# One core, sparse attention feeding a feed-forward layer: a head of feed-forward steps for the second chunk, and two small adds moved from GpSimd to VectorE

## The chip, the cores and the metric

The kernel runs on one core of a Trainium2 chip, as one program. The metric is device time in microseconds (us) of one execution. The core's engines run side by side, each taking its own instructions in order: TensorE (PE in the rows, its weight loads PEld), VectorE (DVE), ScalarE (ACT), GpSimd (POOL) and SyncE (SP, which here only issues DMAs).

## The reference, cut to what matters

Attention of 4 batches x 8 heads over 768 positions of 64, where a query sees 4 sink positions and a window of 128; then a feed-forward layer 512 -> 2048 -> 512 on all 3072 tokens, with a piecewise quadratic in the middle.

```python
scores = np.matmul(q, k.transpose(0, 1, 3, 2)) / np.sqrt(D)
scores = np.where(is_sink | in_window, scores, -1e9)
a = np.exp(scores - np.max(scores, axis=-1, keepdims=True))
a = a / (np.sum(a, axis=-1, keepdims=True) + 1e-09)
x = np.matmul(a, v)                   # then heads side by side: 3072 x 512
h = x @ w_in
g = np.where(h >= 1, h, np.where(h <= -1, 0, (h + 1) ** 2 / 4))
out = g @ w_out
```

## The kernel before

The tokens are cut into eight chunks of 384 (a batch, first or second half). A chunk's attention is eight units, one for each head; its feed-forward work is `moe_steps`: four `split` steps (the chunk's activations as a rounded part, ScalarE L596, and a rest, VectorE L597), then for each of 16 blocks `j` four steps `stage1` (L566, twelve matmuls into one PSUM bank `h_ps`, of which there are two) and, two blocks behind, three steps `stage2` (L585). Between them a block's values pass L573, L574 (ScalarE), L575 (VectorE), L576 (ScalarE) and L577 (GpSimd in chunk 0, VectorE later).

Every matmul operand is such a pair of a rounded part and a rest. The weights arrive as 64-bit words and are decoded once, in 16 weight steps, each a DMA (L199) and four VectorE passes over 128 x 1024 with a ScalarE cast ahead of the last: L164, L170, L173, cast L174, L177. Four of them lie in `first_pairs`, the attention of chunk 0, and twelve are spread over chunk 0's feed-forward steps. Below, "weight step 15" is the sixteenth and last; its destination is the last `w` of the decode, and weight step 14's is `wi_150`.

The loop at L641 builds, for chunk c, the list of attention steps of chunk c and of feed-forward steps of chunk c - 1, merged by `spread` in proportion to weights. In pass c == 1 the attention list is four pairs of heads of `pair_steps` (chunk 1, on 64-row operands: scores L422, transposes L455 and L457, sums L486, values L474), and after it the first "native" units, 16 and 17, of chunk 2. TensorE runs exactly in the order in which steps are called (`manual_schedule`). For the other engines a scheduler, at build time, decides the order from its own estimates, so that an edit of the list moves their instructions too.

A native unit's softmax: `scores` (L277) for three query tiles, maximum and shift on VectorE (L281), exponent on ScalarE (L284, which also sums), the 1e-9 on GpSimd (L289), the reciprocal (L290), the two weighted passes (L296, L298), the sink part (L301), all on VectorE; then TensorE's transposes L336 (tiles) and L337 (sinks). GpSimd also forms the rests of the queries (L263), for units 16 to 19 those of the keys (L261), of the values (L314), and of the block values in chunk 0 (L577).

Of the kernel before, what the change touches and what calls it, by code (L numbers as in the profile page):

```python
# [13 lines left out]
ALU = mybir.AluOpType  # L14
# [5 lines left out]
CT = 3  # L20
NSINK = 4
KB = P + NSINK
NCT = DM // P
# [5 lines left out]
NATIVE = 16  # L29
# [11 lines left out]
LEAD = 0.9  # L41
# [8 lines left out]
def attn_ffn(ctx, tc, qk, qkp, vx, vs, par, w_in, w_out, out):  # L50
    nc = tc.nc
# [214 lines left out]
    def scores(u, i):  # L266
        b, h, t0 = u
        qs, k_s = st["qk", u]
        if i == 0:
            st["p", u] = [att.tile([P, CT, 260], F32, name="p"), att.tile([P, 2 * CT], F32, name="stat")]  # L270
        p, stat = st["p", u]
        t = t0 + i
        lo = KB if t == 0 else 0
        c0 = i * KB if t0 else max(0, (i - 1) * KB)
        ps = ps_a.tile([P, 512], F32, name="ps_a")
        for j, q in enumerate(qs):
            nc.tensor.matmul(ps[:, lo:260], lhsT=q[:, i * P:(i + 1) * P], rhs=k_s[:, c0:c0 + 260 - lo],  # L277
                             start=(j == 0), stop=(j == len(qs) - 1))
        peak_i = peak[:, units.index(u), i:i + 1]
        m = (m0, m1, m2)[min(t, 2)]  # L280
        nc.vector.tensor_tensor_reduce(  # L281
            out=p[:, i, lo:260], in0=ps[:, lo:260], in1=m, scale=-0.125, scalar=3.0e38,
            op0=ALU.add, op1=ALU.min, accum_out=peak_i)
        nc.scalar.activation(p[:, i, lo:260], p[:, i, lo:260], AF.Exp, bias=peak_i, scale=-1.0,  # L284
                             accum_out=stat[:, i:i + 1])
        if i < CT - 1:
            return
        st.pop(("qk", u))
        nc.gpsimd.tensor_scalar(stat[:, CT:2 * CT], stat[:, 0:CT], 1.0e-9, None, op0=ALU.add)  # L289
        nc.vector.reciprocal(stat[:, CT:2 * CT], stat[:, CT:2 * CT])  # L290
        i0 = int(t0 == 0)

        for i in range(CT):
            r, own = stat[:, CT + i:CT + i + 1], p[:, i, KB:260]
            if t0 + i == 0:
                nc.vector.tensor_scalar(own, own, r, None, op0=ALU.mult)  # L296
            else:
                nc.vector.tensor_tensor_reduce(out=own, in0=own, in1=p[:, i, 0:P], scale=r, scalar=0.0,  # L298
                                               op0=ALU.add, op1=ALU.add, accum_out=stat[:, i:i + 1])
        sk = att.tile([P, CT * NSINK], F32, name="sk")[:, :(CT - i0) * NSINK]  # L300
        nc.vector.tensor_tensor(sk.rearrange("p (i s) -> p i s", s=NSINK), p[:, i0:, P:KB],  # L301
                                stat[:, CT + i0:2 * CT].unsqueeze(2).broadcast_to([P, CT - i0, NSINK]), op=ALU.mult)
        st["p", u] = (p, sk)
# [186 lines left out]
    def pair_steps(m):  # L490

        a, b = 2 * m - 2, 2 * m - 1
        sc = [(0.45, lambda i=i: pair_scores(m, i)) for i in range(CT)] if m < NATIVE // 2 else [(0.0, lambda: None)] * CT
        steps = [(0.0, lambda: pair_load(m + 1))] if m + 1 < NATIVE // 2 else []
        if m < NATIVE // 2:
            steps.append((0.0, lambda: pair_values(m)))
        tp = [(0.35, lambda u=u, i=i: early_transp(u, i)) for u in (a, b) for i in range(2)]
        pv = [(0.65, lambda: pair_r(m - 1)), (1.2, lambda: pair_av(m - 1)())]
        dg = [(0.0, lambda: pair_sums(m))] if m < NATIVE // 2 else []
        if m % (H // 2) == 0:  # L500
            return steps + tp[:3] + sc[:1] + tp[3:] + pv[:1] + sc[1:2] + pv[1:] + sc[2:] + dg
        return steps + tp[:1] + sc[:1] + tp[1:] + sc[1:2] + pv + sc[2:] + dg
# [38 lines left out]
    units = [(b, h, t0) for b, t0 in chunks for h in range(H)]  # L541

    def attn_steps(n):
        us = {k: units[n - k] for k in (-1, 0, 1, 2) if 0 <= n - k < len(units)}
        steps = []
        if n == NATIVE:
            steps.append((0.0, lambda: load(us[0])))
        if -1 in us:
            steps.append((0.0, lambda: load(us[-1])))
        if 1 in us and n - 1 >= NATIVE:  # L550
            steps.append((0.0, lambda: values(us[1])))
        steps += [(0.22, lambda i=i: scores(us[0], i)) for i in range(CT) if 0 in us]
        steps += [(0.43, lambda: transp(us[1]))] if 1 in us and n - 1 >= NATIVE else []
        steps += [(1.0, lambda: av(us[2]))] if 2 in us and n - 2 >= NATIVE else []
        if n in CHECK:
            steps.append((0.0, lambda: recheck(n - CHECK[0], n)))
        return steps
# [41 lines left out]
    def moe_steps(row0, tail):  # L599

        x = xpool.tile([P, 2, NCT, CT * P], F32R, name="x")
        o_ps, hs = [], {}
        steps = [(0.0, lambda ct=ct: split(x, ct)) for ct in range(NCT)]
        second = tail[:]
        for j in range(NJ):
            if j < LAG:
                steps += second[j * CT:(j + 1) * CT]
            steps += [(0.49, lambda j=j, ct=ct: stage1(x, j, ct, hs, row0)) for ct in range(NCT)]
            if j >= LAG:
                steps += [(0.65, lambda j=j - LAG, tt=tt: stage2(o_ps, hs, j, tt, row0)) for tt in range(CT)]  # L610
        tail[:] = [(0.65, lambda j=j, tt=tt: stage2(o_ps, hs, j, tt, row0)) for j in range(NJ - LAG, NJ)
                   for tt in range(CT)]
        return steps

    def spread(a, b, lead=1.0):

        wa, wb = (sum(w for w, _ in s) for s in (a, b))
        steps, n, da, db = [], 0, 0.0, 0.0
        for step in b:
            while n < len(a) and da * lead * wb <= db * wa:  # L620
                steps.append(a[n])
                da += a[n][0]
                n += 1
            steps.append(step)
            db += step[0]
        return steps + a[n:]
# [14 lines left out]
    for c in range(len(chunks)):  # L641
        n1 = min(H * (c + 1), len(units)) + 2
        if c == 1:
            attn = [step for m in range(5, 9) for step in pair_steps(m)]
            attn += [step for n in range(NATIVE, n1) for step in attn_steps(n)]
        elif c > 1:
            attn = [step for n in range(n0, n1) for step in attn_steps(n)]
        n0 = n1
        for _, f in spread(attn, prev, LEAD) if c else [(0.0, first_pairs)]:
            f()  # L650
        if c == 1:
            early.close()
            chk.append(fast.enter_context(tc.tile_pool(name="chk", bufs=2)))
        b, t0 = chunks[c]
        prev = moe_steps(b * S + t0 * P, tail)
        if c == 0:
            prev = spread([(1.0, f) for f in wsteps[WFIRST:]], prev, WLEAD)
# [141 lines left out]
```

## Time and profile before

| | us |
|---|---|
| median of 3 runs | 713.11 |
| lowest and highest | 712.43, 714.05 |
| the profiled execution, whole | 713.94 |
| its span, first to last instruction | 712.2 |
| PE busy in the span | 688.1 |
| DVE busy | 512.9 |
| ACT busy | 489.4 |
| POOL busy | 296.2 |

A busy PE is one with a matmul under way, whose ends are modelled, so that two that follow each other overlap in the rows; the time from one start to the next says how fast it issues. A bracket behind a row is the engine's idle time ahead of it and what ended that. "ACTq" marks a DMA issue on that engine's queue.

### The profile page before, as it was taken

To read this page: it belongs to the slowest core of one execution; us is meant where nothing else is said; L and a number is where in the kernel's file an instruction comes from. 1 tells how busy PE (TensorE), PEld (TensorE's weight loads), DVE (VectorE), ACT (ScalarE), POOL (GpSimd) and SP (SyncE) were. 2 spreads that over 40 slices of the span, in tenths; PEclk is the share of its full clock that TensorE was granted. 3 is DMA by queue.
4 is the path that set the end of the run, shared out by engine and by line. 5 is a ranking of instruction groups with operands and counts; after the bars stand their busy time and mean duration, and the time that the engine had idled before them with its cause. 6 is when DMAs were issued, how large, how long until landed. Compare 5 with 4: busy or idle time off the path is not lost.

```text
span 712.2 us, 12391 instructions
## 1 busy us (share of the span) xinstructions
PE 688.1 (97%) x3937; PEld 611.2 (86%) x3937; DVE 512.9 (72%) x1405; ACT 489.4 (69%) x1265; POOL 296.2 (42%) x509
## 2 busy tenths in 40 slices
PE   6799998999999999999999999999999999999996
PEld 4577877999999999999899898999989999989995
DVE  7978998886767768788777778778776777632221
ACT  5876666686768777786777777777766866544332
POOL 2012444754544554456564455636554444400000
PEclk9999999999999999999999999999999999999999
DMA  8845533132144333254433443334422220001001
GB/s 266 297 159 188 177 126 102 46 103 58 50 138 136 104 111 120 73 165 128 118 99 108 118 126 118 118 119 123 123 56 60 88 60 17 8 1 46 0 1 49
DMA packets 44841, 73.04 MB, mean 103 GB/s; under 512 B 13024, under 2 KB 29408, under 8 KB 44768
## 3 DMA queue, kind: packets, MB, share of 16 engines
q1 hardware_dynamic: 41504, 59.59, 27.5%
q10 hardware_dynamic: 3264, 12.58, 4.9%
q8 instruction: 33, 0.54, 0.3%
q14 instruction: 40, 0.33, 0.1%
HBM read 65.87 MB, written 6.29 MB: 101 GB/s over the span
## 4 chain that ended last, share of the span: by engine, by line
PE 73%; DVE 11%; ACT 6%; DMA 3%; POOL 2%; issue 2%; SPq 0%; ACTq 0%; POOLq 0%; DVEq 0%
PE o_ps L585 30%; PE h_ps L566 30%; PE ps_a L383 4%; PE ps_a L277 4%; PE ps_a L336 2%; DVE bits L170 1%; DMA again<-w_in 1%; DVE bits L173 1%; DVE p L298 1%; ACT p L284 1%; DMA w<-w_in 1%; DVE g L575 1%; DVE gl L577 1%; POOL q_l L263 1%; PE ps_a L474 1%
## 5 line engine op out<-in xcount | busy, mean ns | idle before, releaser
L566 PE MATMUL h_ps<-x,wi 128*128 128x384 f32 x1536 | 310.5, 341 | 0.0
L566 PEld LDWEIGHTS h_ps<-x,wi 128*128 128x128 f32 x1536 | 264.3, 189 | 9.8 <-issue 1.5
L585 PE MATMUL o_ps<-w,gh 128*128 128x512 f32 x768 | 243.9, 398 | 0.0
L585 PE MATMUL o_ps<-w,gl 128*128 128x512 f32 x384 | 151.2, 394 | 0.9 <-DVE gl L577 0.9
L585 PEld LDWEIGHTS o_ps<-w,gh 128*128 128x128 f32 x768 | 134.1, 188 | 16.5 <-issue 1.7
L575 DVE SCALAR_TENSOR_TENSOR g<-g,h_ps 128x384 f32<-128x384 f32 x128 | 70.4, 550 | 63.9 <-ACT g L574 62.2
L573 ACT ACTIVATE g<-h_ps,half 128x384 f32<-128x384 f32 x128 | 73.9, 578 | 58.0 <-PE h_ps L566 56.9
L263 POOL TENSOR_TENSOR q_l<-r,q_h 128x384 fp32r<-128x384 f32 x48 | 50.7, 1056 | 132.1 <-ACT q_h L262 123.2
L576 ACT CAST gh<-g 128x384 fp32r<-128x384 f32 x128 | 65.6, 512 | 57.3 <-DVE g L575 56.8
L585 PEld LDWEIGHTS o_ps<-w,gl 128*128 128x128 f32 x384 | 72.0, 188 | 18.6 <-DVE gl L577 1.3
L577 DVE TENSOR_TENSOR gl<-g,gh 128x384 fp32r<-128x384 f32 x112 | 68.6, 612 | 25.3 <-ACT gh L576 24.3
L284 ACT ACTIVATE p<-p,peak 128x260 f32<-128x260 f32 (+1 forms) x144 | 71.4, 496 | 17.5 <-DVE peak L281 16.8
L261 DVE TENSOR_TENSOR k_s<-k_r,k_s 64x524 fp32r<-64x524 f32 (+1 forms) x44 | 46.4, 1054 | 40.0 <-ACT k_s L259 39.9
L574 ACT ACTIVATE g<-g 128x384 f32<-128x384 f32 x128 | 66.9, 523 | 2.1
L281 DVE CUSTOM_DVE_ANT_0 p<-ps_a,m 128x260 f32<-128x260 f32 (+1 forms) x144 | 56.6, 409 | 15.9 <-PE ps_a L277 15.1
L347 POOL TENSOR_SCALAR_AFFINE_SELECT pt<-pt 128x384 fp32r<-128x384 f32 (+1 forms) x96 | 51.0, 531 | 18.2 <-DVE pt L340 16.3
L298 DVE CUSTOM_DVE_ANT_0 p<-p,stat 128x128 f32<-128x128 f32 x128 | 55.4, 477 | 0.0
L345 POOL TENSOR_SCALAR_AFFINE_SELECT pt<-pt 128x384 fp32r<-128x384 f32 (+1 forms) x96 | 50.4, 525 | 7.1 <-ACT pt L339 3.0
L577 POOL TENSOR_TENSOR gl<-g,gh 128x384 fp32r<-128x384 f32 x16 | 22.6, 1415 | 69.0 <-ACT gh L576 65.5
L383 PEld LDWEIGHTS ps_a<-pt,v_s 128*128 128x128 f32 x304 | 46.6, 188 | 2.2
L383 PE MATMUL ps_a<-pt,v_s 128*128 128x256 f32 (+1 forms) x304 | 47.0, 275 | 0.0
L277 PE MATMUL ps_a<-k_s,q_h 128*128 128x260 f32 (+1 forms) x144 | 40.0, 278 | 0.9 <-DVE sk L342 0.9
(147 smaller groups left out, 977.2 us busy)
## 6 DMA issues: line engine op xcount, KB each, us to landing
r<-qk SPq DMA_DIRECT2D x48, 192.0 KB
k_r<-qk SPq DMA_DIRECT2D x32, 262.0 KB
again<-w_in SPq DMA_DIRECT2D x16, 512.0 KB
again<-w_out SPq DMA_DIRECT2D x16, 512.0 KB
w<-w_in ACTq DMA_DIRECT2D x6, 1024.0 KB
w<-w_out ACTq DMA_DIRECT2D x6, 1024.0 KB
out<-o SPq DMA_DIRECT2D x23, 256.0 KB
r<-vx SPq DMA_DIRECT2D x32, 128.0 KB
```

The source lines that it names most:

```text
L263: nc.gpsimd.tensor_tensor(q_l, q_r, q_h.bitcast(F32), op=ALU.subtract)
L277: nc.tensor.matmul(ps[:, lo:260], lhsT=q[:, i * P:(i + 1) * P], rhs=k_s[:, c0:c0 + 260 - lo], start=(j == 0), stop=(j == len(qs) - 1))
L284: nc.scalar.activation(p[:, i, lo:260], p[:, i, lo:260], AF.Exp, bias=peak_i, scale=-1.0, accum_out=stat[:, i:i + 1])
L298: nc.vector.tensor_tensor_reduce(out=own, in0=own, in1=p[:, i, 0:P], scale=r, scalar=0.0, op0=ALU.add, op1=ALU.add, accum_out=stat[:, i:i ...
L383: nc.tensor.matmul(z, lhsT=w, rhs=y, start=(n == 0), stop=(n == len(mms) - 1))
L566: nc.tensor.matmul(h_ps[:, :T], lhsT=w_i[j][:, w, ct * P:(ct + 1) * P], rhs=x[:, y, ct], start=(ct == 0 and n == 0), stop=(ct == NCT - 1 a ...
L573: nc.scalar.activation(g, h_ps[:, :T], AF.Relu, bias=half, scale=0.5)
L574: nc.scalar.activation(g, g, AF.Square)
L575: nc.vector.scalar_tensor_tensor(g, g, 1.0, h_ps[:, :T], op0=ALU.min, op1=ALU.max)
L576: nc.scalar.copy(gh, g)
L577: (nc.gpsimd if row0 == GL_POOL else nc.vector).tensor_tensor(gl, g, gh.bitcast(F32), op=ALU.subtract)
L585: nc.tensor.matmul(o_ps[tt], lhsT=gg[:, tt * P:(tt + 1) * P], rhs=w_o[j][:, w], start=(j == 0 and n == 0), stop=(j == NJ - 1 and n == 2))
```

## The change

In pass c == 1 the first nine entries of the feed-forward list are called ahead of everything else: one weight step, the four `split` steps and the four `stage1` steps of block 0, and the rest is spread as before. And for units 16 and 17 the 1e-9 is added by VectorE.

```diff
-        nc.gpsimd.tensor_scalar(stat[:, CT:2 * CT], stat[:, 0:CT], 1.0e-9, None, op0=ALU.add)
+        (nc.vector if units.index(u) < NATIVE + 2 else nc.gpsimd).tensor_scalar(stat[:, CT:2 * CT], stat[:, 0:CT], 1.0e-9,
+                                                                               None, op0=ALU.add)
...
-        for _, f in spread(attn, prev, LEAD) if c else [(0.0, first_pairs)]:
+        head = NCT + NCT + 1 if c == 1 else 0
+        for _, f in prev[:head] + spread(attn, prev[head:], LEAD) if c else [(0.0, first_pairs)]:
```

Below, lines from L290 on of the changed kernel stand one further down than before, those behind L646 two.

TensorE where pass c == 1 begins, behind the scores of head pair 4 (`ident,p` is a transpose of pair 4, `wi_143` and `wi_144` are `stage1` of blocks 0, 1 and 2, 3). Before:

```order
L422 MATMUL ps_a<-k_s,q_h 128x260
L455 MATMUL ps_a<-ident,p 128x128 x3
L566 MATMUL h_ps<-x,wi_143 128x384 x3
L422 MATMUL ps_a<-k_s,q_h 128x128 x2
L566 MATMUL h_ps<-x,wi_143 128x384 x9
```

Now:

```order
L423 MATMUL ps_a<-k_s,q_h 128x260
L567 MATMUL h_ps<-x,wi_143 128x384 x12
L456 MATMUL ps_a<-ident,p 128x128 x3
L567 MATMUL h_ps<-x,wi_143 128x384 x9
L423 MATMUL ps_a<-k_s,q_h 128x128 x2
```

All twelve matmuls of block 0 now stand ahead of the first transposes.

VectorE at the end of that pass, from unit 17's first maximum (`m_109`) to unit 16's first weighted pass (L296 before, L297 now). Before:

```order
L177 TENSOR_TENSOR wi_150<-bits_1259,wi_150 128x2x512
L281 ISA p,peak<-ps_a,m_109 128x128
L281 ISA peak 128x1
L281 ISA p,peak<-ps_a,m_107 128x260
L281 ISA peak 128x1
L281 ISA p,peak<-ps_a,m_106 128x260
L281 ISA peak 128x1
L290 RECIPROCAL stat<-stat 128x3
L296 TENSOR_SCALAR p<-p,stat 128x128
```

Now:

```order
L164 TENSOR_SCALAR bits_1335<-w 128x1024
L170 SCALAR_TENSOR_TENSOR bits_1335<-w,bits_1335 128x1024
L281 ISA p,peak<-ps_a,m_107 128x260
L281 ISA peak 128x1
L289 TENSOR_SCALAR stat<-stat 128x3
L281 ISA p,peak<-ps_a,m_106 128x260
L281 ISA peak 128x1
L173 SCALAR_TENSOR_TENSOR bits_1335<-w,bits_1335 128x1024
L291 RECIPROCAL stat<-stat 128x3
L576 SCALAR_TENSOR_TENSOR g<-g,h_ps 128x384
L289 TENSOR_SCALAR stat<-stat 128x3
L297 TENSOR_SCALAR p<-p,stat 128x128
```

Weight step 14's last pass (`wi_150`) has gone from this stretch to a place ahead of unit 16's maxima; three passes of weight step 15 (`bits_1335`) and one block's L576 have come into it, and the two adds.

TensorE behind unit 17's last scores. Before:

```order
L277 MATMUL ps_a<-k_s,q_l 128x260
L585 MATMUL o_ps<-w,gh 128x512 x2
L585 MATMUL o_ps<-w,gl 128x512
L336 MATMUL ps_a<-ident,p 128x128 x3
L337 MATMUL ps_a<-ident,sk 8x128
L585 MATMUL o_ps<-w,gh 128x512 x2
L585 MATMUL o_ps<-w,gl 128x512
L566 MATMUL h_ps<-x,wi_150 128x384 x12
```

Now:

```order
L586 MATMUL o_ps<-w,gh 128x512 x2
L586 MATMUL o_ps<-w,gl 128x512
L337 MATMUL ps_a<-ident,p 128x128 x3
L338 MATMUL ps_a<-ident,sk 8x128
L567 MATMUL h_ps<-x,wi_150 128x384 x12
```

Three matmuls of `stage2` that stood behind the transposes now stand ahead of them; from `wi_150` on TensorE's order is that of before. SyncE's order is the same throughout.

## Rows read from the trace of the kernel before

**Rows 1.** The page's first part: span, busy time and instructions of each engine.

```profile
span 712.2 us, 12391 instructions
PE 688.1 (97%) x3937; PEld 611.2 (86%) x3937; DVE 512.9 (72%) x1405; ACT 489.4 (69%) x1265; POOL 296.2 (42%) x509
```

**Rows 2.** Stretches (us from the span's start): length, busy time and instructions of PE, PEld, DVE, ACT, POOL, then the granted TensorE clock, the DMA engines' share and GB/s. One from the middle of pass c == 1, two behind its last wait.

```profile
70.00:74.00 4.00, 4.00 (x31) 2.97 (x31) 3.93 (x7) 2.21 (x7) 1.62 (x1) 1.00 1.02 410
...
123.30:126.70 3.40, 3.40 (x12) 3.21 (x11) 3.40 (x10) 1.52 (x4) 2.75 (x3) 0.50 0.24 63
126.70:130.00 3.30, 3.30 (x18) 2.92 (x18) 3.24 (x5) 1.87 (x5) 3.30 (x4) 1.00 0.34 89
```

**Rows 3.** Who waited for whom from 36 to 132 us, PE and then DVE: us in total, times, longest.

```profile
PE ps_a L336 <- DVE p L296: 2.0, 1, 2.0
PE ps_a L455 <- ACT p L438: 1.2, 2, 1.0
...
DVE wi L177 <- ACT wi L174: 3.5, 4, 1.7
```

**Rows 4.** The timeline where pass c == 1 begins, PE and DVE: start, us, engine, line, operation.

```profile
39.90 0.42 DVE L433 CUSTOM_DVE_ANT_0 p<-h_ps,m1n 128x260 f32<-128x260 f32 x1
...
40.95 1.22 DVE L177 TENSOR_TENSOR w<-bits,w 128x1024 fp32r<-128x1024 f32 x1
...
41.30 0.44 PE L455 MATMUL ps_a<-ident,p 128*128 128x128 f32 x2 [0.96 <-ACT p L438]
...
42.09 0.55 DVE L597 TENSOR_TENSOR x<-xn,x 128x384 fp32r<-128x384 f32 x1
...
42.62 1.83 PE L566 MATMUL h_ps<-x,wi 128*128 128x384 f32 x9
...
44.28 0.38 PE L455 MATMUL ps_a<-ident,p 128*128 128x128 f32 x2
```

**Rows 5.** The timeline of PE at the end of the pass.

```profile
116.99 0.22 PE L277 MATMUL ps_a<-k_s,q_h 128*128 128x128 f32 x1
...
119.36 0.40 PE L585 MATMUL o_ps<-w,gl 128*128 128x512 f32 x1
121.71 0.87 PE L336 MATMUL ps_a<-ident,p 128*128 128x128 f32 x3 [1.95 <-DVE p L296]
122.77 0.27 PE L337 MATMUL ps_a<-ident,sk 128*8 128x128 f32 x1 [0.18 <-DVE sk L301]
...
123.82 3.56 PE L566 MATMUL h_ps<-x,wi 128*128 128x384 f32 x12
127.22 0.63 PE L585 MATMUL o_ps<-w,gh 128*128 128x512 f32 x2
...
129.30 2.25 PE L566 MATMUL h_ps<-x,wi 128*128 128x384 f32 x12
131.38 0.63 PE L585 MATMUL o_ps<-w,gh 128*128 128x512 f32 x2
```

**Rows 6.** The timeline of POOL there (the first two belong to unit 18, the third holds the adds of units 16 and 17, the last is unit 19's).

```profile
118.38 1.26 POOL L263 TENSOR_TENSOR q_l<-r,q_h 128x384 fp32r<-128x384 f32 x1 [1.58 <-ACT q_h L262]
119.72 1.02 POOL L261 TENSOR_TENSOR k_s<-k_r,k_s 64x392 fp32r<-64x392 f32 x1
120.82 0.55 POOL L289 TENSOR_SCALAR stat<-stat 128x3 f32<-128x3 f32 x2
...
123.88 1.98 POOL L261 TENSOR_TENSOR k_s<-k_r,k_s 64x392 fp32r<-64x392 f32 x1 [1.19 <-ACT k_s L259]
```

**Rows 7.** The timeline of DVE there, from weight step 14's last pass to the first of weight step 15.

```profile
117.55 1.22 DVE L177 TENSOR_TENSOR wi<-bits,wi 128x1024 fp32r<-128x1024 f32 x1
118.68 0.28 DVE L281 CUSTOM_DVE_ANT_0 p<-ps_a,m 128x128 f32<-128x128 f32 x1
...
121.09 0.18 DVE L290 RECIPROCAL stat<-stat 128x3 f32<-128x3 f32 x1 [1.42 <-POOL stat L289]
121.37 0.29 DVE L296 TENSOR_SCALAR p<-p,stat 128x128 f32<-128x128 f32 x1
121.57 0.35 DVE L298 CUSTOM_DVE_ANT_0 p<-p,stat 128x128 f32<-128x128 f32 x1
...
122.12 0.59 DVE L301 TENSOR_TENSOR sk<-p,stat 128x8 f32<-128x8 f32 x1
122.63 0.68 DVE L164 TENSOR_SCALAR bits<-w 128x1024 int32<-128x1024 int32 x1
```

**Rows 8.** DVE passes beside a POOL operation: the timeline of DVE and, last, of POOL.

```profile
106.12 1.23 DVE L170 SCALAR_TENSOR_TENSOR bits<-w,bits 128x1024 int32<-128x1024 int32 x1
107.38 1.92 DVE L173 SCALAR_TENSOR_TENSOR bits<-w,bits 128x1024 int32<-128x1024 int32 x1
...
124.90 1.04 DVE L296 TENSOR_SCALAR p<-p,stat 128x128 f32<-128x128 f32 x1
...
106.19 2.02 POOL L577 TENSOR_TENSOR gl<-g,gh 128x384 fp32r<-128x384 f32 x1 [2.78 <-ACT gh L576]
```

**Rows 9.** The last weight DMA: its issue in ACT's timeline, then two stretches with columns as in rows 2.

```profile
116.02 0.38 ACTq L199 DMA_DIRECT2D w<-w_out  x1
...
119.00:120.00 1.00, 0.76 (x4) 0.28 (x2) 0.67 (x4) 1.00 (x6) 0.92 (x2) 1.00 1.04 426
120.00:121.00 1.00, 0.00 (x0) 0.00 (x0) 0.00 (x0) 1.00 (x6) 0.91 (x2) 1.00 0.45 157
```

## The prediction, made before the changed kernel was run

> **What bounds the kernel now.** I read the page's first part, then stretches of a few microseconds, the waits, and the timelines where the edited list begins and ends. TensorE is busy for 688.1 of 712.2 us [rows 1], so what counts is where it waits or runs slowly. The pass that is edited lies between about 40 and 123 us. In its middle TensorE is busy all the time while VectorE, with the weight decode, has 0.07 us of 4 left [rows 2]; in the list of waits from 36 to 132 us nothing of weight stands against TensorE but two places [rows 3]. At the pass's beginning it waits for exponents ahead of its transposes: 0.96 us before 41.30 [rows 4]. At its end it waits 1.95 us for unit 16's first weighted pass (L296) and 0.18 us for the sink part [rows 5]. Behind that its granted clock is 0.50, which is 1.2 GHz: the twelve matmuls of block 14 take 3.40 us from start to the next line's start, those of 129.30 only 2.08 [rows 2, 5]. After 126.70 the clock is full and the order of instructions is that of before, so the time moves by what TensorE is early or late when it reaches block 14.
>
> Why it waits at the end: the maxima of unit 16 and 17 are done by 119.7, but the 1e-9 stands on GpSimd behind unit 18's L263 and L261 and starts at 120.82 [rows 6]; VectorE sits idle for 1.42 us until the add is done, then runs L290, L296, L298 twice and L301, whose end at 122.71 releases L337 [rows 7].
>
> **The head.** Block 0's twelve matmuls now stand ahead of the transposes. They need a bank that a maximum frees at 39.90 + 0.42 = 40.32, three parts of the activations that are long there, and the fourth, whose rest (L597) ends at 42.64 [rows 4]. An L566 issues every 2.08 / 12 = 0.173 us [rows 5]: nine are out by 41.9, a tenth waits for nothing new, and the last two wait until 42.64 and are out at 43.0. Before, block 0 was out at 44.28, with 0.9 us of transposes and scores among it: 41.30 to 42.62 is 1.32 us, of which three L566 are 0.52, and one transpose stood at 40.01 (0.1) [rows 4]. Put behind: 43.0 + 0.9 = 43.9, so TensorE gains **0.4 us** there. Bounds: 0, and 0.96, the whole idle time. VectorE's L177 (1.22 us) still stands ahead of L597, so the full 0.96 is not to be had; I keep 0.4.
>
> In the middle the steps are the same and in other places. Moved on TensorE are whole groups; its sum of issue stays. Moved on VectorE are the twelve decodes. There the slack is 3.5 us of waits for the cast between L173 and L177 [rows 3], and the new order often has another instruction between these two, so I take 0; bounds 0 and 1 us, the latter if a late maximum holds a PSUM bank once or twice for as long as L170 takes (1.23 us [rows 8]). SyncE's order is untouched, and ScalarE's DMA issues stay in the same turn among the decode's casts.
>
> **The end of the pass, where the sum is made.** The adds leave GpSimd, so the 1.42 us wait is gone. What is next late on VectorE? Two moves. Weight step 14's last pass (L177, 1.22 us at 117.55 [rows 7]) has gone ahead of unit 16's maxima. Unit 17's first scores, issued at 116.99 before [rows 5], come 0.4 earlier; with unit 16's third maximum just ahead, their maximum should end at about 117.5 and not at 118.96 [rows 7]. But from there to the weighted passes VectorE, which runs in order, now has: L164 0.68, L170 1.23, a maximum 0.42, the add 0.18, a maximum 0.42, L173 1.23, the reciprocal 0.18, one L575 0.55, an add 0.18, L296 0.29, two L298 0.70, L301 0.59. Lengths: L164, L290 (for the adds too), L296, L298, L301 of rows 7; L170 and L173 as the first of rows 8; the maxima as L433 and L575 as L597, of equal width [rows 4]. That is 6.65 us; a row starts some 0.08 us before the one ahead has ended (L296 at 121.37 lasts 0.29, L298 starts at 121.57 [rows 7]), twelve times: 5.7. L301 would end at 117.5 + 5.7 = **123.2**, against 122.71: weight step 15 takes more than the wait gave.
>
> To that comes GpSimd. L173 at 107.38 took 1.92 us, 0.69 more than L170 ahead of it, while an L577 of GpSimd lay from 106.19 to 108.21; L296 at 124.90 took 1.04, 0.75 more than its twin, beside unit 19's L261 [rows 7, 8, 6]. In the old stretch VectorE ran maxima (from PSUM) and waited while GpSimd had its L263 and L261 (1.26 and 1.02 us [rows 6]); now L164, L170, L173 and L296 fall on unit 18's L263 and L261, on the values' rest and on unit 19's L261. Nothing to three such hits, 0 to 2.1 us; I take two, 1.45, since VectorE's passes follow one another there without a break: L301 ends at **124.65**, 1.95 later than before.
>
> The Trainium skill, SBUF — State Buffer, section "SBUF: two separate sides", says that VectorE in its faster modes or with two SBUF inputs and GpSimd share one pair of ports, as a lock held for the whole instruction, and that the loser fully blocks. It speaks against giving VectorE more of such passes just there; the two rows above agree (0.69 and 0.75 us lost). By the rule all three GpSimd operations that meet it would be paid once, an estimate of 2.1 us in place of 1.45, and the sum below would be 715.9.
>
> The last weight DMA is issued with the cast of weight step 14. At 116.02 before, its traffic is over by about 121 [rows 9], so 5 us. By the new order that cast stands behind block 12's L573 on ScalarE, which I place at about 113: the words land at about 118, when L164 wants them at 117.5. VectorE's queue would stand behind L164: unit 17's maxima and all of unit 16's chain. I take 0, since GpSimd's hits and this wait overlap; bounds 0 and 1.
>
> Three matmuls of L585 now stand ahead of L336: nine take 2.08 us (127.22 to 129.30 [rows 5]), so 0.69 us of TensorE's work moves into the wait. L337 starts at 124.7 instead of 122.77, with 0.69 less behind it: 1.95 - 0.69 = **+1.25 us**. The head's 0.4 is in this (it set the 117.5); TensorE's own lead is waited away, from about 119.9 to 123.7. The 1.2 GHz behind the wait is paid as before. If the longer idle time (3.8 us for 1.95) brings a second stretch of it, one such stretch of 3.4 us at half speed is 1.7 more [rows 2]: bounds 0 and 1.7, in the sum 0.
>
> Sum: 713.94 (the profiled execution; its span 712.2 and 1.7 around it) + 1.25 = **715.2**. That execution lies 0.8 above the median 713.11, and the three runs spread over 1.6, about one stretch at 1.2 GHz. I expect each execution after the change to have that stretch, so I count from the profiled one.
>
> **The rivals.** A measurement of this kernel can tell about 0.2%, 1.4 us, from no change: faster is below 711.7, slower above 714.5.
>
> (a) Not slower: GpSimd's operations miss VectorE's passes. Then L301 ends at 123.2, and 0.5 - 0.7 = -0.2: 713.7, or 712.9 if the clock falls no more often than in the median run. For it: before, maxima and L177 met L263 at 118.38 with little loss [rows 6, 7]. Against: L164 and L170 stand back to back at 117.5, when unit 18's operands come to GpSimd. It decides when unit 18's L261 ends before L164 starts.
>
> (b) Faster: the wait becomes so short that the clock stays at 2.4 GHz. L301 would have to end by about 122: -0.7 - 0.7 - 1.7 = -3.1, 710.8. For it: the 1.42 us wait for GpSimd is indeed gone. Against: 5.7 us of VectorE work behind unit 17's first maximum.
>
> (c) Slower by more: a second stretch at 1.2 GHz, 715.2 + 1.7 = 716.9, with the DMA's wait up to 717.9. For it: the idle time doubles. Against: half of it may lie in the stretch that is slow anyway.
>
> (d) The head does nothing: the scheduler or a bank keeps block 0 where it was. TensorE's order is the list's, so only the bank could; the sum would be 0.4 more.
>
> **How the numbers follow.** Forecast, 714.5 to 716.2 with (d) in it: 0.47. (a): 0.32. (b): 0.07. (c): 0.14. Slower is the forecast, less a little below its edge, and (c): 0.58; same is (a) and that little: 0.34; faster is (b) and a sliver of (a): 0.08. The range takes in (a), with the clock as in the median run and 0.5 us less, and the most of (c): 712.4 to 717.4; outside lie (b) and the tail of (c) and of a late middle, some 0.15.
>
> **What would show it.** Head: block 0's matmuls start at about 40.4, with a gap before the last two. Middle: TensorE busy 4.00 of 4. End: VectorE's wait for GpSimd's add gone; L164, L170 and L173 ahead of L296, one or two of them over 1.6 us; TensorE's wait before L336 3 to 4 us in place of 1.95, L337 at 124 to 125, then the clock at 0.50. The forecast is wrong if the wait at L336 is below 2 us or moves nowhere near VectorE, or if TensorE waits in the middle for a PSUM bank.

## The result, and the profile after

The changed kernel takes 719.3 us (median of 4 runs, 718.87 to 720.2), the kernel before 713.58 us beside it: a ratio of 1.0082, 95% interval 1.0068 to 1.0097. It is slower, as forecast, but the profiled execution, 720.2 us against 713.94, lost 6.3 us where the sum had 1.25, and the time lies outside the range of 712.4 to 717.4.

The page's first part after, to be held against [rows 1]: TensorE's busy time grew by 2.0 us while the span grew by 6.3, so most of the loss is waiting.

```profile
span 718.5 us, 12393 instructions
PE 690.1 (96%) x3937; PEld 612.0 (85%) x3937; DVE 512.3 (71%) x1407; ACT 489.9 (68%) x1265; POOL 291.2 (41%) x507
```

The waits from 36 to 140 us, PE's, then one of DVE's (us in total, times, longest). Against [rows 3], the wait ahead of unit 16's transposes is 4.9 us instead of 2.0, and VectorE waits for a weight DMA, which it did not before; its wait for GpSimd's add is gone.

```profile
PE ps_a L337 <- DVE p L297: 4.9, 1, 4.9
...
DVE bits L164 <- DMA w<-w_out: 1.1, 1, 1.1
```

TensorE's timeline at the head of the pass, then at its end (to [rows 4] and [rows 5]). At the head, ten matmuls of block 0 leave at 40.21 and two wait for the fourth activation part, just as forecast; the transposes come at 42.97, behind all twelve. At the end, unit 17's first scores come at 117.13, which is 0.14 us later than before; L337 comes at 125.59 where L336 came at 121.71, and the twelve matmuls of block 15 at 133.92 for 129.30: 4.62 us late.

```profile
40.21 2.00 PE L567 MATMUL h_ps<-x,wi 128*128 128x384 f32 x10 [0.54 <-DVE peak L434]
42.51 0.62 PE L567 MATMUL h_ps<-x,wi 128*128 128x384 f32 x2 [0.30 <-DVE x L598]
42.97 0.49 PE L456 MATMUL ps_a<-ident,p 128*128 128x128 f32 x3
...
117.13 0.33 PE L277 MATMUL ps_a<-k_s,q_h 128*128 128x128 f32 x1 [0.19 <-DVE peak L281]
...
120.31 0.39 PE L586 MATMUL o_ps<-w,gl 128*128 128x512 f32 x1
125.59 0.81 PE L337 MATMUL ps_a<-ident,p 128*128 128x128 f32 x2 [4.89 <-DVE p L297]
126.95 0.45 PE L337 MATMUL ps_a<-ident,p 128*128 128x128 f32 x1 [0.55 <-DVE sk L302]
...
127.26 4.19 PE L567 MATMUL h_ps<-x,wi 128*128 128x384 f32 x12
...
133.92 2.25 PE L567 MATMUL h_ps<-x,wi 128*128 128x384 f32 x12
```

Why unit 16's first weighted pass (L297) is so late stands in the timelines of VectorE, of GpSimd in the four rows behind it, and of ScalarE's queue in the last row, the issue of weight step 15's DMA (to [rows 7], [rows 6] and [rows 9]). Unit 17's first maximum (117.69) is done at 117.97; then VectorE stands for 1.10 us behind L164, until weight step 15's words land; L164, L170, L297 and the second L299 are all longer than without a neighbour (0.68 and 0.29 in [rows 7], 1.23 in [rows 8], 0.34 in the first L299). Each of the four lies beside one of these GpSimd passes: L164 beside L263, which runs until 119.49, L170 beside the L261 of 119.57, L297 beside that of 124.44, the second L299 beside L578.

```profile
117.69 0.28 DVE L281 CUSTOM_DVE_ANT_0 p<-ps_a,m 128x128 f32<-128x128 f32 x1
...
119.08 0.96 DVE L164 TENSOR_SCALAR bits<-w 128x1024 int32<-128x1024 int32 x1 [1.10 <-DMA w<-w_out]
120.07 1.94 DVE L170 SCALAR_TENSOR_TENSOR bits<-w,bits 128x1024 int32<-128x1024 int32 x1
...
122.70 1.21 DVE L173 SCALAR_TENSOR_TENSOR bits<-w,bits 128x1024 int32<-128x1024 int32 x1
...
124.43 1.10 DVE L297 TENSOR_SCALAR p<-p,stat 128x128 f32<-128x128 f32 x1
125.46 0.34 DVE L299 CUSTOM_DVE_ANT_0 p<-p,stat 128x128 f32<-128x128 f32 x1
...
125.73 1.07 DVE L299 CUSTOM_DVE_ANT_0 p<-p,stat 128x128 f32<-128x128 f32 x1
...
126.73 0.15 DVE L302 TENSOR_TENSOR sk<-p,stat 128x8 f32<-128x8 f32 x1
...
118.47 1.02 POOL L263 TENSOR_TENSOR q_l<-r,q_h 128x384 fp32r<-128x384 f32 x1
119.57 1.36 POOL L261 TENSOR_TENSOR k_s<-k_r,k_s 64x392 fp32r<-64x392 f32 x1
...
124.44 1.01 POOL L261 TENSOR_TENSOR k_s<-k_r,k_s 64x392 fp32r<-64x392 f32 x1
125.65 1.00 POOL L578 TENSOR_TENSOR gl<-g,gh 128x384 fp32r<-128x384 f32 x1 [0.20 <-ACT gh L577]
...
114.15 0.38 ACTq L199 DMA_DIRECT2D w<-w_out  x1
```

Stretches after, with the columns of [rows 2]. Behind the wait TensorE runs at 1.2 GHz (granted clock 0.50) for 6.8 us, against 3.4 before; the first row shows TensorE busy all the time in a stretch of the middle.

```profile
70.00:74.00 4.00, 4.00 (x30) 3.42 (x29) 4.00 (x7) 2.03 (x6) 1.03 (x1) 1.00 0.49 200
125.69:132.51 6.82, 6.27 (x19) 5.46 (x20) 4.81 (x15) 1.95 (x5) 4.03 (x6) 0.50 0.23 66
132.51:136.00 3.49, 3.49 (x19) 3.21 (x18) 0.62 (x2) 0.93 (x3) 2.19 (x3) 1.00 0.20 56
```

### The profile page after: what moved, and what is told of

Same layout as the page of the kernel before. It is cut to its first block, busy times and chain, and to the rows that moved or that the text cites. A ratio compares the mean times of both kernels' runs of the same rounds, so it can differ in the third digit from the quotient of the medians.

```text
span 718.5 us, 12393 instructions
## 1 busy us (share of the span) xinstructions
PE 690.1 (96%) x3937; PEld 612.0 (85%) x3937; DVE 512.3 (71%) x1407; ACT 489.9 (68%) x1265; POOL 291.2 (41%) x507
## 4 chain that ended last, share of the span: by engine, by line
PE 68%; DVE 12%; ACT 7%; DMA 6%; POOL 3%; issue 3%; SPq 0%; ACTq 0%; POOLq 0%; DVEq 0%
PE o_ps L586 28%; PE h_ps L567 28%; PE ps_a L384 4%; PE ps_a L277 3%; DMA again<-w_out 2%; PE ps_a L337 2%; DVE p L299 1%; DMA r<-qk 1%; ACT p L284 1%; DVE gl L578 1%; POOL q_l L263 1%; DMA w<-w_in 1%; DVE bits L170 1%; DVE g L576 1%; ACT q_h L262 1%
## 5 line engine op out<-in xcount | busy, mean ns | idle before, releaser
L586 PE MATMUL o_ps<-w,gh 128*128 128x512 f32 x768 | 244.6, 399 | 0.0
L586 PE MATMUL o_ps<-w,gl 128*128 128x512 f32 x384 | 151.3, 394 | 0.4 <-DVE gl L578 0.4
L586 PEld LDWEIGHTS o_ps<-w,gh 128*128 128x128 f32 x768 | 134.2, 189 | 16.4 <-issue 2.0
L576 DVE SCALAR_TENSOR_TENSOR g<-g,h_ps 128x384 f32<-128x384 f32 x128 | 70.4, 550 | 65.2 <-ACT g L575 63.4
L263 POOL TENSOR_TENSOR q_l<-r,q_h 128x384 fp32r<-128x384 f32 x48 | 50.2, 1047 | 133.3 <-ACT q_h L262 126.4
L586 PEld LDWEIGHTS o_ps<-w,gl 128*128 128x128 f32 x384 | 72.2, 188 | 18.6 <-DVE gl L578 1.2
L578 DVE TENSOR_TENSOR gl<-g,gh 128x384 fp32r<-128x384 f32 x112 | 68.7, 613 | 25.5 <-ACT gh L577 24.5
L261 DVE TENSOR_TENSOR k_s<-k_r,k_s 64x524 fp32r<-64x524 f32 (+1 forms) x44 | 46.4, 1055 | 42.4 <-ACT k_s L259 42.3
L299 DVE CUSTOM_DVE_ANT_0 p<-p,stat 128x128 f32<-128x128 f32 x128 | 56.6, 486 | 0.0
L348 POOL TENSOR_SCALAR_AFFINE_SELECT pt<-pt 128x384 fp32r<-128x384 f32 (+1 forms) x96 | 48.9, 510 | 17.6 <-DVE pt L341 15.7
L346 POOL TENSOR_SCALAR_AFFINE_SELECT pt<-pt 128x384 fp32r<-128x384 f32 (+1 forms) x96 | 50.5, 526 | 8.0 <-ACT pt L340 2.9
L578 POOL TENSOR_TENSOR gl<-g,gh 128x384 fp32r<-128x384 f32 x16 | 21.1, 1318 | 68.7 <-ACT gh L577 64.8
```

The source lines that it names most:

```text
L263: nc.gpsimd.tensor_tensor(q_l, q_r, q_h.bitcast(F32), op=ALU.subtract)
L576: nc.vector.scalar_tensor_tensor(g, g, 1.0, h_ps[:, :T], op0=ALU.min, op1=ALU.max)
L578: (nc.gpsimd if row0 == GL_POOL else nc.vector).tensor_tensor(gl, g, gh.bitcast(F32), op=ALU.subtract)
L586: nc.tensor.matmul(o_ps[tt], lhsT=gg[:, tt * P:(tt + 1) * P], rhs=w_o[j][:, w], start=(j == 0 and n == 0), stop=(j == NJ - 1 and n == 2))
```

## The experiments

Theory 1: the head moves weight step 15 into unit 16's softmax chain on VectorE, and that place, with its DMA and GpSimd's neighbours, is the loss. Theory 2: the loss is the two adds that VectorE took over. Theory 3, beside theory 1: part of the loss is the lower clock behind the longer wait. Each time is a median beside runs of the kernel before on the same chip.

### e1_head_alone and e2_add_alone: the two halves of the change

e1, against the changed kernel:

```diff
-        (nc.vector if units.index(u) < NATIVE + 2 else nc.gpsimd).tensor_scalar(...)
+        nc.gpsimd.tensor_scalar(...)
```

> The head of eight steps alone, with all the adds back on GpSimd. Theory 1: the loss comes from the last weight step, which the head moves into unit 16's chain of softmax passes on VectorE (its transfer, its passes and what GpSimd's passes add to them); that order is the same here, so 719 us (717.5 to 720.5), with a TensorE wait of 4 to 6 us ahead of unit 16's transposes. Theory 2: the loss comes from the two adds that VectorE took over; then this is as fast as the kernel before, 713.6 us (712.4 to 714.6).

e2, against the changed kernel:

```diff
-        head = NCT + NCT + 1 if c == 1 else 0
-        for _, f in prev[:head] + spread(attn, prev[head:], LEAD) if c else [(0.0, first_pairs)]:
+        for _, f in spread(attn, prev, LEAD) if c else [(0.0, first_pairs)]:
```

> The two adds on VectorE alone, without the head. Theory 1: the last weight step stays where it was and the wait of VectorE for GpSimd's add (1.42 us in the kernel before) is gone, so 711.5 us (710 to 712.5), with TensorE's wait ahead of unit 16's transposes shorter than the 1.95 us of the kernel before. Theory 2 (the adds cost): 719 us (717.5 to 720.5).

e1 took 717.19 us, ratio 1.0060 (1.0040 to 1.0079); e2 712.58 us, ratio 0.9997 (0.9984 to 1.0010). The head alone brings the loss or most of it, the adds alone bring none: theory 2 falls. e1 came out a little under the range of theory 1; its profiled execution, the fastest of four (715.34 us, the others 716.62 to 718.37), has a wait of 3.92 us and half as long a stretch at the lower clock. Its stretch and its timelines, PE's and then DVE's, show one reason for the shorter wait: unit 16's L296 takes 0.27 us instead of 1.10, because it is done before GpSimd's L261 starts (124.09), which stands behind the adds there.

```profile
124.93:128.34 3.41, 2.94 (x10) 2.89 (x11) 3.38 (x9) 0.89 (x2) 2.88 (x4) 0.50 0.38 110
...
123.97 0.66 PE L336 MATMUL ps_a<-ident,p 128*128 128x128 f32 x2 [3.92 <-DVE p L296]
...
123.64 0.27 DVE L296 TENSOR_SCALAR p<-p,stat 128x128 f32<-128x128 f32 x1
```

e2's profile has a wait of 1.12 us there and no stretch at the lower clock behind it (granted clock 1.00 from 119 to 132 us); TensorE reaches block 15 at 126.37, 2.9 us earlier than before. Yet the run is no faster than the kernel before: the expectation of a gain failed. Of the 2.9 us, 1.2 are gone by the first matmul of chunk 1's block 0 (134.52 against 136.25): in between TensorE waits 0.94 us for one of chunk 0's block values, which GpSimd still has to form (L578), a wait that the kernel before does not have.

```profile
120.63 0.94 PE L337 MATMUL ps_a<-ident,p 128*128 128x128 f32 x3 [1.12 <-DVE p L297]
```

### e3_step15_late and e5_step15_between: weight step 15 elsewhere

Against the changed kernel; in both, the old place in the list stays empty:

```diff
-            prev = spread([(1.0, f) for f in wsteps[WFIRST:]], prev, WLEAD)
+            prev = spread([(1.0, f) for f in wsteps[WFIRST:-1] + [lambda: None]], prev, WLEAD)
...
+        # e3: at the end of unit 17's list; e5: at its beginning
+        steps += [(0.0, wsteps[-1])] if n == NATIVE + 1 else []
```

> The changed kernel with one thing undone: the last weight step is called behind unit 16's transposes (in unit 17's list), its old place in the list stays empty, and so all the other weight steps stand where they did. Theory 1: the wait of 4.9 us ahead of unit 16's transposes goes to under 1 us; 709.5 to 712 us. Rival (the head itself costs on TensorE, by its place or by the clock, or the feed-forward weights come late now): 717 us or more.

> The changed kernel with the last weight step called at the head of unit 17's list: its first three passes stand behind the whole chain of unit 16 on VectorE and are mixed into the chain of unit 17. With the step called too late, its weights arrived 4.1 us behind the feed-forward's matmuls that read them; here they are written some 5 us earlier. Theory 1 (the step has two deadlines, unit 16's transposes ahead of it and the feed-forward blocks 14 and 15 behind it, and the changed kernel misses the first): no wait over 1.2 us of TensorE at either place, 709.5 to 712 us. Rival: the passes of the step cost VectorE the same time wherever they stand, the wait only moves to unit 17's transposes or to the blocks 14 and 15; 714.5 us or more.

e3 took 716.85 us, ratio 1.0049 (1.0029 to 1.0069). The wait ahead of unit 16's transposes fell from 4.9 to 0.5 us as theory 1 said, but the time lies close to the rival's 717 us (the ten executions between 714.8 and 720.1, the profiled one 719.92): the weights now come too late for blocks 14 and 15. In the timeline of PE the first L587 that reads them waits for the cast and then for the last pass, 4.06 us in all, and the long durations behind that are the lower clock again (0.50 for 6.8 us from 134.66 on):

```profile
133.90 0.49 PE L587 MATMUL o_ps<-w,gh 128*128 128x512 f32 x1 [3.00 <-ACT w L174]
135.45 0.80 PE L587 MATMUL o_ps<-w,gh 128*128 128x512 f32 x1 [1.06 <-DVE w L177]
136.05 0.63 PE L587 MATMUL o_ps<-w,gl 128*128 128x512 f32 x1
```

So the step has two deadlines. e5 puts it between them: 712.37 us, ratio 0.9999 (0.9984 to 1.0014). The whole loss is gone with the head and the adds still in, which shows theory 1. The rows, PE then DVE: a wait of half a microsecond, L164 behind unit 16's chain (its L302 is at 122.55) and with no wait for the DMA. TensorE reaches block 15 at 127.19, 2.1 us earlier than before, and here too it then waits for a block value of GpSimd's (L580).

```profile
122.15 0.93 PE L337 MATMUL ps_a<-ident,p 128*128 128x128 f32 x3 [0.52 <-DVE p L297]
...
132.99 0.50 PE L588 MATMUL o_ps<-w,gl 128*128 128x512 f32 x1 [0.79 <-POOL gl L580]
...
122.63 0.69 DVE L164 TENSOR_SCALAR bits<-w 128x1024 int32<-128x1024 int32 x1
```

712.37 lies just above the range given: relative to the kernel before it is no gain.

### e4_fill, e8_fill12 and e10_before_fill: the clock by itself

Against the changed kernel, in `transp` ahead of the transposes (28 in e4, 12 in e8; e10 puts 10 into the kernel before):

```diff
+        for _ in range(28 if units.index(u) == NATIVE else 0):
+            nc.tensor.matmul(ps[:, :T], lhsT=w_i[0][:, 0, 0:P], rhs=w_i[0][:, 0, 0:T], start=True, stop=True)
```

> The changed kernel with 28 extra matmuls of 384 columns put on TensorE ahead of unit 16's transposes; their result is overwritten and used by nothing, so this is added work in the time in which TensorE waits. VectorE's chain is as long as before. Theory 3: part of the loss (about 3.4 us of the 6.8 us at half clock behind the wait) is the lower clock that follows the wait; with TensorE kept at work it stays at the full clock, 714.5 to 717 us. Rival: the clock's fall costs nothing of its own, or comes anyway; 718.5 to 721 us.

> The changed kernel with 12 extra matmuls of 384 columns ahead of unit 16's transposes (result overwritten and unused, added work), so that some 2.7 us of the 4.9 us wait is left. Theory 3 with two stretches: behind a wait of 2 to 4 us the clock is at 1.2 GHz for 3.4 us, behind one of 4.9 us for twice that; here one stretch of about 3.4 us, and so 1.7 us less than the changed kernel: 717 to 718.5 us. Rival: the length of the stretch does not hang on the wait's length: 6.8 us at half clock and 719 to 720.5 us.

> The kernel before with 10 extra matmuls of 384 columns ahead of unit 16's transposes (result overwritten and unused, added work), which fill most of its wait of 1.95 us there. Theory 3: the stretch of 3.4 us at 1.2 GHz that follows the wait in the kernel before is gone, which is worth up to 1.7 us: 711 to 712.5 us, with the granted clock 1.00 from 120 to 132 us. Rival: the clock falls anyway, or the extra matmuls cost as much: 713 us or more.

e4 took 714.23 us, ratio 1.0014 (0.9994 to 1.0035), just under the range of theory 3. VectorE's chain is as long as in the changed kernel and TensorE does 5 us more work, and the loss is nearly gone. PE's timeline: the extra matmuls fill the wait, the twelve of block 14 issue at full speed, and those of block 15 come at 131.97, though the pass's end began 0.6 us later than in the profile of the changed kernel.

```profile
121.12 5.02 PE L335 MATMUL ps_a<-wi 128*128 128x384 f32 x28
126.20 0.66 PE L339 MATMUL ps_a<-ident,p 128*128 128x128 f32 x2
...
127.72 2.33 PE L569 MATMUL h_ps<-x,wi 128*128 128x384 f32 x12
...
131.97 2.25 PE L569 MATMUL h_ps<-x,wi 128*128 128x384 f32 x12
```

Of the 6.0 us between the two spans (718.5 and 712.5), 1.95 are visible here, or 2.5 with the later start. The rest comes later: from the first matmul of chunk 1's block 0 to TensorE's last `stage2` matmul it took 566.2 us in e4's profile, 570.4 in the changed kernel's, and 568.7 in that of its second run below. TensorE's order there is the same in all of them, and none has a stretch at 1.2 GHz in it, so this part differs between executions and is not put down to the clock.

e8 took 717.27 us, ratio 1.0066 (1.0041 to 1.0091): in the range of theory 3, but not for its reason. The wait left was 2.82 us, and the stretch at 1.2 GHz was as long as behind 4.89, as the rows show. Nor was time saved at this place: from TensorE's last L588 ahead of the extra matmuls (120.58) to block 15 (133.87) it took 13.29 us, in the two profiles of the changed kernel 13.61 and 12.98. The time is not clear of that of the changed kernel on the same chip (below): the intervals overlap. "The longer the wait, the longer the stretch" falls.

```profile
125.88 0.81 PE L339 MATMUL ps_a<-ident,p 128*128 128x128 f32 x2 [2.82 <-DVE p L297]
...
125.28:132.10 6.82, 5.67 (x18) 5.08 (x19) 5.30 (x15) 1.77 (x5) 4.58 (x7) 0.50 0.27 75
```

e10 took 712.13 us, ratio 0.9992 (0.9981 to 1.0003), in the range of theory 3 but not clear of the kernel before. With 0.24 us of its wait left, the kernel before keeps the full clock (the stretch below, with [rows 2] at 0.50 from 123.30), and reaches block 15 at 127.02, 2.3 us sooner. Of that 2.3 us the run shows 1 us or less.

```profile
121.34 0.87 PE L338 MATMUL ps_a<-ident,p 128*128 128x128 f32 x3 [0.24 <-DVE p L296]
...
124.00:128.00 4.00, 4.00 (x22) 3.61 (x21) 4.00 (x9) 1.77 (x5) 3.93 (x5) 1.00 0.37 99
```

### e7_loads_late and e9_few_passes: GpSimd beside the chain

e7, against the changed kernel:

```diff
-        if -1 in us:
+        if -1 in us and n not in (NATIVE, NATIVE + 1):
             steps.append((0.0, lambda: load(us[-1])))
...
+        if n in (NATIVE, NATIVE + 1):
+            steps.append((0.0, lambda: load(us[-1])))
```

> The changed kernel with the loads of units 17 and 18 called at the end of their unit's list rather than at its head, so that GpSimd's passes of 1.0 to 1.4 us on the keys and queries fall elsewhere. The last weight step stays in unit 16's chain. Theory 1 with contention as a term (VectorE's passes there are about 2.5 us longer where GpSimd works beside them): the wait of 4.9 us shrinks to 2.5 to 3.5 us and the second half of the stretch at the lower clock goes with it; 714 to 717 us. Rival: the contention is no cause of length there, 718.5 to 721 us; or the later loads make unit 17's or 18's scores wait, over 721 us.

e9, against the changed kernel, for units 17 and 18 alone:

```diff
-        eng.tensor_tensor(k_s[D:P], k_r[D:P], k_s[D:P].bitcast(F32), op=ALU.subtract)
...
-        nc.gpsimd.tensor_tensor(q_l, q_r, q_h.bitcast(F32), op=ALU.subtract)
+        nc.scalar.copy(q_l, q_r)
```

> The changed kernel with GpSimd's four passes on the keys and queries of units 17 and 18 left out: the keys' pass is not done, and the queries' low part is written by a copy on ScalarE instead (so the scores of these two units are computed from other numbers; the work on TensorE and VectorE is the same in kind and length). The last weight step stays in unit 16's chain. Theory 1 with contention as a term: of the chain's passes the first three that GpSimd's passes lengthened (0.96, 1.94 and 1.10 us in the changed kernel) go to about 0.7, 1.2 and 0.3 us, the wait from 4.9 to 2.5 to 3.5 us, the run by as much, to 716.5 to 717.8 us. Rival (those passes are long for another reason): the wait stays at 4.5 us or more and the time at 718 us or more.

e7 took 719.36 us, ratio 1.0100 (1.0078 to 1.0121), in the rival's range, and tells nothing of contention, since the edit did not do what was meant: unit 18's passes on GpSimd stayed where they were (L164 0.90 and L170 1.94 us, as in the changed kernel), only unit 19's came earlier and the values' rest later, and they met others of the chain. In its timelines of VectorE and GpSimd, L297 is short and the L299 behind it long:

```profile
123.84 0.27 DVE L297 TENSOR_SCALAR p<-p,stat 128x128 f32<-128x128 f32 x1
124.03 1.10 DVE L299 CUSTOM_DVE_ANT_0 p<-p,stat 128x128 f32<-128x128 f32 x1
...
123.98 1.01 POOL L261 TENSOR_TENSOR k_s<-k_r,k_s 64x392 fp32r<-64x392 f32 x1
```

e9 removes such passes: 716.31 us, ratio 1.0051 (1.0035 to 1.0068), a little under its range. VectorE's order around the chain is that of the changed kernel but for unit 17's add, which comes behind it (L302 here is L297 there, L307 is L302). L164 starts at the same time as there (119.13), and the first two passes shrink to their lengths without a neighbour, the third by half; TensorE's wait, in the last row, is 2.66 us. That shows contention as a term: from the start of L164 to the end of the sink part it is 5.77 us (119.13 to 124.90) against 7.80 (119.08 to 126.88), 2.0 us less.

```profile
119.13 0.69 DVE L164 TENSOR_SCALAR bits<-w 128x1024 int32<-128x1024 int32 x1 [0.30 <-DMA w<-w_out]
119.86 1.23 DVE L170 SCALAR_TENSOR_TENSOR bits<-w,bits 128x1024 int32<-128x1024 int32 x1
...
123.43 0.51 DVE L302 TENSOR_SCALAR p<-p,stat 128x128 f32<-128x128 f32 x1
...
124.74 0.16 DVE L307 TENSOR_TENSOR sk<-p,stat 128x8 f32<-128x8 f32 x1
...
124.00 0.66 PE L342 MATMUL ps_a<-ident,p 128*128 128x128 f32 x2 [2.66 <-DVE p L302]
```

### after_again, e11_between_pool_add and e12_between_again

The first is the changed kernel, the last the kernel of e5 with more rounds; e11 is e5 with e1's edit, so that the head is all that is left of the change.

> The changed kernel itself once more, on the same chip as these runs: 719.3 us (718 to 720.5), with the wait of 4.9 us and 6.8 us at half clock in its profile. If it comes out at 717 us or so, the difference of 2 us between it and the head alone was the spread of executions and not the adds.

> The head kept, the last weight step behind unit 16's chain as in e5, and all the adds back on GpSimd: VectorE's order around unit 16 is then that of the kernel before, and the head is all that is left of the change. If the add on VectorE is worth its wait once the step is out of the way: the 1.4 us wait for GpSimd is back, TensorE's wait ahead of unit 16's transposes is 1.5 to 2.5 us and the clock falls behind it, 713 to 714.5 us. Rival (the add's place matters for nothing): 711.5 to 712.5 us, as e5.

> The kernel of e5 once more, with more rounds, as the version that could beat both: head and adds as in the changed kernel, and the last weight step at the head of unit 17's list. Theory 1: 711 to 712.5 us, 0.1 to 0.3% under the kernel before. Rival: what it gains at unit 16 (2 to 3 us) is used up by other waits, and it is as fast as the kernel before, 712.5 to 714 us.

The changed kernel took 718.54 us, ratio 1.0080 (1.0057 to 1.0103), in the range expected, with the wait of 4.89 us (to 126.48) and 6.83 us at 1.2 GHz again, which this time began while TensorE still waited. Its interval overlaps that of e1, so whether the adds on VectorE cost anything beside the head is not settled.

```profile
125.26:132.09 6.83, 5.06 (x16) 4.56 (x17) 5.92 (x17) 2.13 (x4) 4.87 (x7) 0.50 0.27 75
```

e11 took 712.29 us, ratio 0.9990 (0.9978 to 1.0002), e12 713.14 us, ratio 0.9997 (0.9983 to 1.0011). Both times fit the rivals. With the adds back on GpSimd, e11's VectorE waits for them only 0.47 us (1.42 in [rows 7]) and TensorE 0.88. The head and the adds are both worth nothing that can be measured once the step is out of the way, and no version that was run beats the kernel before by more than the measurement can tell.

```profile
121.44 0.87 PE L336 MATMUL ps_a<-ident,p 128*128 128x128 f32 x3 [0.88 <-DVE p L296]
...
120.82 0.18 DVE L290 RECIPROCAL stat<-stat 128x3 f32<-128x3 f32 x1 [0.47 <-POOL stat L289]
```

## Why the prediction was wrong in size

**The head** was right where it begins: block 0 from 40.21 with a gap ahead of the last two, the transposes behind it, its two waits 0.84 us together where before TensorE waited 0.96 and 0.19. In the middle no wait of TensorE is longer than 0.2 us. But the lead did not last to unit 17's first scores: the sum had them 0.4 us earlier, they came 0.14 later (117.13 for 116.99). That the head is worth nothing in the end was in the sum too, since TensorE's lead is waited away.

**The mechanism at the end** was right: GpSimd's wait gone, weight step 15's passes in its place ahead of unit 16's weighted passes, a longer wait, and then the lower clock. What failed is the step "L301 ends at 124.65": its like, L302, ended at 126.88, 2.23 us later. By terms:

- *The last weight DMA*, "I take 0, since GpSimd's hits and this wait overlap", was 1.10 us. The 5 us from issue to use were right (114.15 to 119.08), but the cast of weight step 14 stood at 114.09 and not at about 113. The two do not overlap: the wait ends when the words land, and what GpSimd adds comes behind that, to the passes that the wait held up; in e9, without two of GpSimd's passes there, L164 starts at the same time. The bound of 1 was the value.
- *Contention*, two hits for 1.45, was four: 0.28 for L164, 0.71 for L170, 0.81 for L297 and 0.72 for the second L299, together 2.52 us. e9 took 2.0 us of it away. The sum had named four GpSimd operations, bounded them at three hits and taken two. Three of the four did hit; the values' rest (L315) did not, and the fourth hit came from block values on GpSimd (L578), which were not among them.
- Unit 17's first maximum ended 0.48 later than the 117.5 taken, and the sink part took 0.15 in place of 0.59 (that row of [rows 7] had a GpSimd pass, L314, beside it). These two cancel: 0.48 + 1.10 + (2.52 - 1.45) - 0.44 = 2.21.

**TensorE behind the wait.** The sinks' transpose started at 127.19 where I had 124.7, 2.49 us more than the +1.25 of the sum and 4.42 later than before. Block 14 came 3.44 late (127.26 for 123.82): the three L585 that no longer stand between had taken 1.03 us, in part at 1.2 GHz, and not the 0.69 that the sum took off. From there to block 15 it took 6.66 us instead of 5.48, and this 1.18 is the price of the second part of the stretch at 1.2 GHz, which the sum had at 0 and rival (c) at 1.7. From the sum on: 1.25 + 2.49 - 0.30 + 1.18 = 4.62. e4 shows that with TensorE kept at work the whole stretch goes. Rival (c) had this and the DMA's wait, and up to 717.9; with four hits in place of two it would have come to 719.0.

**What the sum did not have.** Between there and the last row of TensorE the profiled execution lost another 1.45 us: that L586 starts at 711.25, its like before at 705.18. In the second profile of the changed kernel it starts at 709.82, which is 4.64 late. So this part differs between executions of one kernel and is no steady cost of the change; in what little waits it lies was not followed up.

**Rivals.** (a) asked GpSimd's passes to miss VectorE's; only e9, which removes them, comes near, and it is still slower, since the step itself stays in the chain. (b)'s condition (a short wait and the full clock) was reached in e2, e5, e10 and e11, and its 710.8 was not: the 2 to 3 us gained at block 15 in e2 and e10 came to 1 us or less in the medians. A part of the gain, 1.2 us in e2 and 0.8 in e10, is lost again before chunk 1's block 0, at the wait for GpSimd's block value; where the rest goes is open. Open too is what decides between a stretch of 3.4 and one of 6.8 us at the lower clock.

**The rule weighed.** The Trainium skill, SBUF — State Buffer, section "SBUF: two separate sides", has VectorE and GpSimd share one pair of ports as a lock held for a whole instruction. The runs agree with it: the maxima, which read PSUM, keep their 0.28 beside L578, the passes from SBUF lose up to 0.8 us, and without GpSimd's passes they lose less or nothing. In the six profiles in which L164 starts while unit 18's L263 still runs (e1, e4, e7, e8 and the two of the changed kernel) it takes 0.78 to 1.02 us, and in each it ends 0.55 or 0.56 us after L263 does, as a pass would that waits for the other's end. Counting every GpSimd operation that meets such a pass, as that rule asks, would have been nearer than my two.

## What to carry to other kernels

A step inserted at the head of a merged list moves everything behind it: look in the new order for the heaviest thing that changed places on the engine that is waited for (here a weight decode that entered a softmax chain), and give that thing both its deadlines. Where a wait holds up a pass that others lengthen, add the wait and the lengthening, and count every operation of the neighbour engine that can lie there, also those that the edit does not touch. A microsecond gained at one place is not a microsecond of the run: the gains of 2 to 3 us at block 15 could hardly be seen in the time, and a part of them went in TensorE's next wait, for an engine that had not held it up there before.

## What the hardware showed that I had not expected

The granted clock fell behind waits as short as 1.95 us (3.4 us at 1.2 GHz, [rows 2, 5]) and stayed at 2.4 GHz behind 1.12 us (e2) and 0.88 us (e11); behind 2.66 us (e9) and 3.92 us (e1) the stretch was 3.4 us, behind 2.82 us (e8), 4.57 us (e7) and 4.89 us it was 6.8. Work that computes nothing of use, put into the wait, kept the clock up: with 5 us of it the changed kernel was 0.7% faster (714.23 against 719.3 us, each beside the kernel before on its own chip), of which the traces show some 2 to 2.5 us where the clock had been low.

Such a stretch is not bound to the place of the edit. Twelve of the fourteen profiles have one in chunk 0's attention too, somewhere between 19 and 38 us (3.4 us long, in e11 6.8; in the kernel before from 34.52 to 37.93), so that part of the spread between executions is the clock's.
